# Sigmoid attention with an MLP behind it: prologue splits and maxima move off GpSimd, and float32 scores use 64 array rows per head

## The chip, the cores and the metric

The kernel runs on one core of a Trainium2 chip. The core has a matrix engine (TensorE, in the profile PE for the multiplications and PEld for its weight loads), VectorE (DVE), ScalarE (ACT), GpSimd (POOL) and SyncE (SP, which here only starts transfers). Each engine takes its own instructions in the order in which they were written down for it. The metric is the device time of one execution in microseconds; lower is better. The kernel before takes 1218.87 us (median of 3 runs, 1217.56 to 1221.67).

## The reference

```python
def _attn_ref(q, k, v):                 # q, k, v: (8, 12, 448, 64) float32
    scale = 1.0 / np.sqrt(q.shape[-1])
    scores = scale * np.matmul(q, k.transpose(0, 1, 3, 2)) - np.log(S)
    attn = 1.0 / (1.0 + np.exp(-scores))          # a sigmoid, no row sums
    return np.matmul(attn, v).astype(np.float32)

def _moe_ref(x, w_in, w_out):           # x: (3584, 768), w_in: 768 x 2048, w_out: 2048 x 768
    h = x @ w_in
    g = np.where(h >= 1, h, np.where(h <= -1, 0.0, (h + 1) ** 2 / 4))
    return (g @ w_out).astype(np.float32)
```

The attention output, transposed to (batch * seq, heads * head_dim), is `x`. Everything has to hold float32 accuracy. The weights arrive as float64.

## The kernel before, in words

**Blocks and pairs.** The work is cut into 8 blocks, one for each batch entry (448 tokens). Two heads make a pair, so a block has 6 pairs and the whole program 48. A pair is done in four pieces: three of 128 keys and one of 64 keys for both heads together (the "mid" piece). For a piece PE makes the scores (`psc`), ACT the sigmoid, and PE adds attention times v into `pav`. When a pair is done, `pav` is copied to `x32`, and VectorE takes its largest absolute value (`xm`).

**Precision.** Nearly every product is made of three float16 products: a number is scaled by a power of two, split into a high float16 part (ACT, a copy that rounds) and a low one (VectorE, scaled number minus high part), and the products high*high, low*high and high*low are added up. The scale comes from a maximum, or a sum that bounds it. Pairs 0 to 7 (`NFULL`) are multiplied in float32 without a split. Pairs 8 to 13 (`NHALF`) have q and k split and the rest in float32; later pairs are split throughout, and q, k and v each need a sum of absolutes, a scale and three GpSimd steps (lines 358 to 360): scale in place, round to the high part, subtract.

**Float32 pairs before the change.** The four buffers of `full` (`NFB = 4`) hold q for both heads on 128 partitions, v, and k twice: once with head 0 alone (the lower 64 partitions zeroed by a memset) and once with head 1 alone. A score matmul of one head therefore runs over 128 array rows, half of them multiplying by zero.

**Weights.** `w_in` and `w_out` come in 16 chunks of 128 x 768 each, as 64-bit words. `Weight.convert` makes float32 of one chunk: an absolute value on ACT (line 215), a lower clamp (line 217 on GpSimd, or line 225 on VectorE with the maximum taken on the way), then three bit operations on VectorE (lines 230, 233, 236). Where GpSimd clamps, a sum of absolutes on ACT (line 209) stands in for the maximum. `split` then makes the two float16 parts, either with ACT and VectorE (lines 275, 276) or with GpSimd scaling, ACT rounding and GpSimd subtracting (lines 271 to 273).

**MLP.** For a block, `up` (line 699) makes h chunk by chunk, `bend` applies the bent square and splits the result (ACT lines 712 and 715, VectorE lines 713, 714 and 716 (`GPOOL = 1` leaves the last on VectorE)), and `down` (line 733) multiplies by `w_out`. Block 0 and 1 do this plainly. From block 2 on (`SB = 2`) the up product goes through seven products of half size (`up_blocks`, line 665), whose weight combinations `mix` computes once, during block 1, and stores in DRAM (`blocks`); `load_set` brings them back.

**What sets the order.** The python code interleaves the pieces of the next block's attention with the MLP units of this one: `step(at)` issues piece `at`, `units` are the MLP units, and constants such as `WI_A`, `B0`, `LAST` and `MIX0` say at which unit which piece, weight chunk or mix step is written. A scheduler then orders each engine's instructions by its own estimate of times, with priorities lent by `tc.high_priority` (`WI_PRIO`, `X_PRIO`, `Q_PRIO`). Only the SP queue of the opening follows the written order. Block 0's MLP needs `finish_x(0)`: the largest of all six `xm`, a scale, and the split of `x32` (lines 500 and 501). For later blocks `start_blocks` and `finish_blocks` do the same at MLP unit `last`.

So there is an opening (weights converted and split, pairs 0 to about 17, the MLP of blocks 0 and 1, the mixing) and then a regular part, blocks 2 to 7.

Of the kernel before, what the change touches and what calls it, by code (L numbers as in the profile page):

```python
# [66 lines left out]
def sigmoid_attention_mlp(ctx: ExitStack, tc: tile.TileContext, first_qvk, qkv, w_in, w_out, out_t):  # L67
# [102 lines left out]
    class Weight:  # L170
# [30 lines left out]
        def convert(self):  # L201
# [11 lines left out]
            if f < NFC:  # L213
                a = self.f32(f)
                nc.scalar.activation(a, self.words_of(f)[1].bitcast(F32), AF.Abs)
                if f in self.summed:
                    nc.gpsimd.tensor_scalar(out=a, in0=a, scalar1=HIGH_MIN, scalar2=None, op0=ALU.max)
# [67 lines left out]
    NFB = 4  # L285
    full = ghl.rearrange("p f h n -> p (f h n)").bitcast(F32).rearrange("p (b t n) -> p b t n", b=NFB, t=4)
    for i in range(NFB):
        nc.vector.memset(full[D:, i, 2, :], 0.0)
        nc.vector.memset(full[:D, i, 3, :], 0.0)
# [47 lines left out]
    def prep_b(p):  # L337
        if not NFULL <= p < NPAIR or not first_time("split", p):
# [17 lines left out]
        for t, dst in enumerate(parts):  # L356
            rt, hi = r[:, t * S : 2 * S + VW if t == 2 else (t + 1) * S], dst[:, 0, :]
            nc.gpsimd.tensor_scalar(out=rt, in0=rt, scalar1=s[:, t : t + 1], scalar2=1.0, op0=ALU.mult, op1=ALU.mult)  # L358
# [14 lines left out]
    def scores(todo):  # L373

        tiles = []
        for i in todo:
# [5 lines left out]
            if p < NFULL:  # L382
                r = ready[p][0]
                for j in range(2):
                    out = psc[j * D : (j + 1) * D, 0, :S] if mid else psc[:, j, :S]
                    nc.tensor.matmul(out, r[:, 2 + j, w], r[:, 0, :], start=True, stop=True)  # L386
# [35 lines left out]
    def weigh(i, psc):  # L422
# [5 lines left out]
        sqk = 1.0 / math.sqrt(D) if p < NFULL else ready[p][2]  # L428
# [19 lines left out]
    def av(i):  # L448
# [30 lines left out]
        if mid:  # L479
            if p < NFULL + NHALF:  # L480
                nc.scalar.activation(x32[:, hp, :], pav[:, :S], AF.Copy)
            else:
# [1 line left out]
                nc.vector.tensor_scalar(
                    out=x32[:, hp, :], in0=pav[:, :S], scalar1=inv[:, 2:3], scalar2=1.0 / ATT, op0=ALU.mult, op1=ALU.mult
                )
# [450 lines left out]
```

## Time and profile before

| of the profiled execution | |
|---|---|
| its own time | 1220.22 us |
| its span (first to last instruction) | 1218.2 us |
| median of 3 other runs | 1218.87 us |
| busy PE, DVE, ACT, POOL | 1169.6, 883.8, 686.7, 495.5 us |
| first `up` matmul of block 0 (line 699) | at 88.45 us |
| first `up` matmul of block 1 (line 699) | at 242.27 us |
| first `up_blocks` matmul of block 2 (line 665) | at 428.36 us |

The last three rows are starts in the timeline and cut the span into stages; all stages below are taken between them. Busy time is the time in which at least one instruction of an engine ran. A matmul's recorded duration is longer than its share of the array's time, since consecutive matmuls overlap; start-to-start times tell what one costs.

### The profile page before, as it was taken

The numbers are of one execution on the slowest core, as the hardware profiler recorded it, in microseconds if no ns is written. First come the engines' busy times: TensorE is split into PE (matmuls) and PEld (weight loads), VectorE is DVE, ScalarE is ACT, GpSimd is POOL, SyncE is SP. The second block draws the span as 40 slices with busy tenths as digits, with TensorE's granted clock in tenths as the row PEclk, the third lists the DMA queues.
The fourth block names the chain that finished last, engine by engine and source line by source line (L and its number), as shares of the span: only waits on it lengthen the run. The fifth ranks groups of instructions, "written<-read, shape, count | busy, mean of one in ns | idle before, by whom it ended". The sixth has DMA issues, their size and how long they took to land.

```text
span 1218.2 us, 20267 instructions
## 1 busy us (share of the span) xinstructions
PE 1169.6 (96%) x7662; PEld 681.2 (56%) x7662; DVE 883.8 (73%) x1756; ACT 686.7 (56%) x1137; POOL 495.5 (41%) x508
## 2 busy tenths in 40 slices
PE   7978879999989999999999999999999999999998
PEld 2323333344444577556774577556774578557954
DVE  6879997799696479845985579845995579844830
ACT  6867657455464277743785377743785378621410
POOL 2567977555455134532354134532354234210000
PEclk9989989899999999999999999999999999999999
DMA  9844314414644136520654136520654136301400
GB/s 324 301 156 149 128 42 153 137 60 150 230 163 151 56 138 231 175 93 26 241 189 140 57 138 225 181 94 25 237 187 145 59 138 207 136 31 64 180 16 31
DMA packets 57217, 170.01 MB, mean 140 GB/s; under 512 B 8736, under 2 KB 37920, under 8 KB 50976
## 3 DMA queue, kind: packets, MB, share of 16 engines
q1 hardware_dynamic: 55392, 159.29, 38.1%
q10 hardware_dynamic: 1728, 9.44, 2.2%
q8 instruction: 60, 0.98, 0.3%
q14 instruction: 37, 0.30, 0.1%
HBM read 126.94 MB, written 23.40 MB: 123 GB/s over the span
## 4 chain that ended last, share of the span: by engine, by line
PE 70%; DVE 13%; POOL 7%; DMA 4%; issue 3%; ACT 2%; SPq 1%; POOLq 0%; ACTq 0%
PE po L733 31%; PE ph L665 22%; PE pav L475 8%; PE psc L395 3%; PE psc L386 2%; PE psc L404 2%; PE psc L390 1%; DVE g L713 1%; POOL w_in_sb L271 1%; DMA raw<-qkv 1%; DVE w_out_sb L233 1%; DVE ghl L716 1%; DVE mixs L623 1%; DMA blocks<-mixs 1%; POOL hl L360 1%
## 5 line engine op out<-in xcount | busy, mean ns | idle before, releaser
L733 PE MATMUL po<-ghl,w_out_sb 128*128 128x448 f16 x2304 | 451.5, 354 | 0.9 <-DVE g L714 0.5
L733 PEld LDWEIGHTS <-w_out_sb 128*128 128x128 f16 x2304 | 221.4, 98 | 222.7 <-issue 23.7
L665 PE MATMUL ph<-w_in_sb 128*128 128x224 f16 x3024 | 303.1, 259 | 1.5 <-DMA w_in_sb<-blocks 1.5
L665 PEld LDWEIGHTS <-w_in_sb 128*128 128x128 f16 x3024 | 285.4, 98 | 23.1 <-issue 17.3
L358 POOL TENSOR_SCALAR raw<-raw,qkv_s 128x448 f32<-128x448 f32 (+1 forms) x114 | 98.3, 874 | 434.6 <-DVE qkv_i L130 207.8
L434 ACT ACTIVATE psc<-psc,nls,sqk 128x896 f32<-128x896 f32 (+1 forms) x136 | 129.5, 971 | 131.2 <-PE psc L404 121.3
L443 DVE SCALAR_TENSOR_TENSOR ahl<-psc,ahl 128x896 f16<-128x896 f32 (+1 forms) x170 | 152.8, 899 | 49.7 <-ACT ahl L442 47.5
L442 ACT ACTIVATE ahl<-psc 128x896 f16<-128x896 f32 (+1 forms) x170 | 125.9, 765 | 37.0 <-DVE ahl L443 35.0
L699 PE MATMUL ph<-xhl,w_in_sb 128*128 128x448 f16 x576 | 120.3, 368 | 9.6 <-DVE g L714 8.0
L743 DVE TENSOR_SCALAR o<-po,od 128x448 f32<-128x448 f32 x48 | 32.6, 681 | 108.5 <-PE po L733 107.7
L475 PE MATMUL pav<-ahl,v 128*64 128x448 f16 x748 | 101.1, 366 | 0.0
L674 DVE TENSOR_TENSOR xhl<-ph,xhl 128x224 f32<-128x224 f32 x240 | 88.0, 384 | 17.7 <-PE ph L665 13.7
L699 PEld LDWEIGHTS <-w_in_sb 128*128 128x128 f16 x576 | 57.1, 101 | 77.9 <-issue 30.4
L332 ACT ACTIVATE dump<-raw 128x448 f16<-128x448 f32 (+1 forms) x108 | 63.6, 589 | 65.4 <-DMA raw<-qkv 62.9
L716 DVE TENSOR_TENSOR ghl<-g,ghl 128x448 f16<-128x448 f32 x128 | 91.0, 726 | 6.3 <-ACT ghl L715 5.9
L715 ACT ACTIVATE ghl<-g 128x448 f16<-128x448 f32 x128 | 72.4, 571 | 35.9 <-DVE g L714 35.0
L360 POOL TENSOR_TENSOR hl<-raw,hl 128x448 f16<-128x448 f32 x80 | 89.3, 1134 | 0.0
L713 DVE SCALAR_TENSOR_TENSOR g<-g,rk 128x448 f32<-128x448 f32 x112 | 84.3, 771 | 2.9 <-ACT g L712 2.2
L712 ACT ACTIVATE g<-xhl,hr,ihr 128x448 f32<-128x448 f32 x96 | 67.9, 753 | 31.9 <-DVE xhl L674 31.5
L395 PE MATMUL psc<-qk 128*128 128x448 f16 x252 | 67.6, 356 | 5.9 <-DVE ahl L443 4.3
L386 PE MATMUL psc<-ghl 128*128 128x448 f32 (+1 forms) x128 | 53.7, 596 | 12.7 <-ACT a L431 6.9
L714 DVE SCALAR_TENSOR_TENSOR g<-xhl,ihs,g 128x448 f32<-128x448 f32 x96 | 63.0, 677 | 0.0
(167 smaller groups left out, 1312.7 us busy)
## 6 DMA issues: line engine op xcount, KB each, us to landing
w_in_sb<-blocks SPq DMA_DIRECT2D x48, 1344.0 KB, 6.3
raw<-qkv SPq DMA_DIRECT2D x34, 704.0 KB, 6.8
qk<-hl SPq DMA_DIRECT2D x320, 56.0 KB, 2.0
w_out_sb<-w_in SPq DMA_DIRECT2D x16, 768.0 KB, 9.4
out_t<-o SPq DMA_DIRECT2D x48, 224.0 KB, 1.9
blocks<-mixs SPq DMA_DIRECT2D x8, 768.0 KB, 4.3
w_out_sb<-w_out ACTq DMA_DIRECT2D x6, 768.0 KB, 4.2
raww<-w_out ACTq DMA_DIRECT2D x6, 768.0 KB, 5.1
```

The lines of the kernel that those rows point to most:

```text
L358: nc.gpsimd.tensor_scalar(out=rt, in0=rt, scalar1=s[:, t : t + 1], scalar2=1.0, op0=ALU.mult, op1=ALU.mult)
L360: nc.gpsimd.tensor_tensor(out=dst[:, 1, :], in0=rt, in1=hi, op=ALU.subtract)
L395: nc.tensor.matmul(out, kq[:, j, 1, w], kq[:, j, 0, :], start=True, stop=False)
L434: nc.scalar.activation(a, a, AF.Sigmoid, bias=nls, scale=sqk)
L442: nc.scalar.activation(hi, x, AF.Copy, scale=ATT)
L443: nc.vector.scalar_tensor_tensor(out=lo, in0=x, scalar=ATT, in1=hi, op0=ALU.mult, op1=ALU.subtract)
L475: nc.tensor.matmul(pav[j * D : (j + 1) * D, :S], *terms[j][t], start=c == 0 and t == 0, stop=mid and t == len(terms[j]) - 1,)
L665: nc.tensor.matmul(out, w[:, wt, wh, c * P : (c + 1) * P], xc[:, xt, c, xh, :], start=j in (0, 2) and c + wh + xh == 0, stop=c == HC - 1 a ...
L699: nc.tensor.matmul(ph[:, :S], w_in_sb[:, f, wh, c * P : (c + 1) * P], xhl[:, c, xh, :], start=c == 0 and wh + xh == 0, stop=c == NCC - 1 a ...
L713: nc.vector.scalar_tensor_tensor(out=g, in0=g, scalar=rt, in1=g, op0=ALU.min, op1=ALU.mult)
L716: (nc.gpsimd if f % GPOOL else nc.vector).tensor_tensor(out=ghl[:, f, 1, :], in0=g, in1=hi, op=ALU.subtract)
L733: nc.tensor.matmul(po[:, :S], w_out_sb[:, f, wh, m * P : (m + 1) * P], ghl[:, f, gh, :], start=f == lo and wh + gh == 0, stop=f == hi - 1 ...
```

## The change

1. **Float32 scores.** `full` has five buffers of three parts (q, v, k) without zeros; a head's scores now take its own 64 partitions of k and q, that is 64 array rows. The memsets go, and a pair is loaded by two transfers where it was three.
2. **Off GpSimd.** In the opening the clamps of `w_in` from chunk 7 on go to VectorE (`CLAMP`). `WO_SUM = 0`: all `w_out` chunks take maximum and clamp in one VectorE instruction (line 236 of the new kernel), without ACT's sum. `POOL_FROM = 6` and `WOP = 6`: `w_in` chunks 4 to 7 and five `w_out` chunks more are split by ACT and VectorE. The q, k and v of pairs 8 to 16 (`QA`) are split by ACT and VectorE, two instructions in place of three. The two additions of each `mix` go to VectorE (`MIXP = 0`).
3. **x32.** For split pairs the copy out of `pav` goes from VectorE to ACT; its factor is made by one tiny VectorE instruction for each pair.
4. **Order.** `LAST` 84 (the regular blocks spread their attention over more MLP units, and `finish_blocks` comes six units later), other times and priorities in the opening, and `down` from block 2 on takes chunks u and u + 8 together.

```diff
-LAST = 78
+LAST = 84
-WI_B = 9
+WI_B = 5
-POOL_FROM = 2
+POOL_FROM = 6
-WO_SUM = 1
-MAX_ACT = 48
+WO_SUM = 0
+MAX_ACT = 47
-MIX0 = 4
+MIX0 = 8
-Q_PRIO = 60
+Q_PRIO = 72
-WI_PRIO = 132
+WI_PRIO = 280
...
-                    nc.gpsimd.tensor_scalar(out=a, in0=a, scalar1=HIGH_MIN, scalar2=None, op0=ALU.max)
+                    (nc.vector if f >= CLAMP else nc.gpsimd).tensor_scalar(
+                        out=a, in0=a, scalar1=HIGH_MIN, scalar2=None, op0=ALU.max
+                    )
...
-            r = full[:, p % NFB]
-            nc.sync.dma_start(out=r[:D, 2, :], in_=first_qvk[p, :D, 2, :])
-            nc.sync.dma_start(out=r[D:, 3, :], in_=first_qvk[p, D:, 2, :])
-            nc.sync.dma_start(out=r[:, 0:2, :], in_=first_qvk[p, :, 0:2, :])
+            r = full[:, slot_of(p)]
+            nc.sync.dma_start(out=r[:, ::2, :], in_=first_qvk[p, :, ::2, :])
+            nc.sync.dma_start(out=r[:, 1, :], in_=first_qvk[p, :, 1, :])
...
+            if p < QA and t != QT:
+                nc.scalar.activation(hi, rt, AF.Copy, scale=s[:, t : t + 1])
+                nc.vector.scalar_tensor_tensor(
+                    out=dst[:, 1, :], in0=rt, scalar=s[:, t : t + 1], in1=hi, op0=ALU.mult, op1=ALU.subtract
+                )
+                continue
...
-                    nc.tensor.matmul(out, r[:, 2 + j, w], r[:, 0, :], start=True, stop=True)
+                    rows = slice(j * D, (j + 1) * D)
+                    nc.tensor.matmul(out, r[rows, 2, w], r[rows, 0, :], start=True, stop=True)
...
-                nc.vector.tensor_scalar(
-                    out=x32[:, hp, :], in0=pav[:, :S], scalar1=inv[:, 2:3], scalar2=1.0 / ATT, op0=ALU.mult, op1=ALU.mult
-                )
+                sv = ready.pop(p)[2][:, 1:2]
+                nc.scalar.activation(x32[:, hp, :], pav[:, :S], AF.Copy, scale=sv)
...
-            nc.gpsimd.tensor_tensor(out=a[:, r], in0=w_in_sb[:, chunk, 0, :], in1=w_in_sb[:, chunk, 1, :], op=ALU.add)
+            (nc.gpsimd if r < MIXP else nc.vector).tensor_tensor(
+                out=a[:, r], in0=w_in_sb[:, chunk, 0, :], in1=w_in_sb[:, chunk, 1, :], op=ALU.add
+            )
...
-        for f in range(lo + 2 * u, lo + 2 * u + 2):
+        pair = (u, u + NFC // 2) if b >= SB else (lo + 2 * u, lo + 2 * u + 1)
+        for f in pair:
...
-                wo.split(split_at, split_at % 2 == 1)
+                wo.split(split_at, split_at % WOP == 1)
```

The scheduler's order moves with it. The first place is GpSimd in the opening. Before, from its first clamp on (line 217 clamps, 271 and 273 split weights, 358 to 360 split q and k; the number behind x counts equal neighbours):

```order
L217 TENSOR_SCALAR w_in_sb<-w_in_sb 128x768 x6
L271 TENSOR_SCALAR w_in_sb<-w_in_sb,wi_s 128x768 x3
L358 TENSOR_SCALAR raw<-raw,qkv_s 128x448 x2
L271 TENSOR_SCALAR w_in_sb<-w_in_sb,wi_s 128x768
L359 TENSOR_SCALAR hl<-raw 128x448 x2
L217 TENSOR_SCALAR w_in_sb<-w_in_sb 128x768
L360 TENSOR_TENSOR hl<-raw,hl 128x448 x2
L358 TENSOR_SCALAR raw<-raw,qkv_s 128x448 x2
L359 TENSOR_SCALAR hl<-raw 128x448 x2
L360 TENSOR_TENSOR hl<-raw,hl 128x448
L217 TENSOR_SCALAR w_in_sb<-w_in_sb 128x768
L360 TENSOR_TENSOR hl<-raw,hl 128x448
```

Now, from its first clamp (line 226) on, up to the split of pair 17, the first pair that it still splits:

```order
L226 TENSOR_SCALAR w_in_sb<-w_in_sb 128x768 x4
L282 TENSOR_SCALAR w_in_sb<-w_in_sb,wi_s 128x768 x8
L284 TENSOR_TENSOR w_in_sb<-w_in_sb 128x768 x8
L434 MEMSET w_in_sb 128x256 x2
L282 TENSOR_SCALAR w_out_sb<-w_out_sb,wo_s 128x768 x2
L284 TENSOR_TENSOR w_out_sb<-w_out_sb 128x768 x2
L282 TENSOR_SCALAR w_out_sb<-w_out_sb,wo_s 128x768
L284 TENSOR_TENSOR w_out_sb<-w_out_sb 128x768
L437 COPY w_in_sb<-hl 64x2x64 x6
L378 TENSOR_SCALAR raw<-raw,qkv_s 128x448 x2
```

These few rows are nearly all that GpSimd does in the opening now; before, the piece shown is only its beginning.

The second place is VectorE just ahead of `finish_x(0)`, whose split of x (line 501) block 0's `up` waits for. Before (line 236 the last bit operation of a chunk, 276 a weight split, 487 the maximum of a finished pair, 496 the maximum over the block):

```order
L487 TENSOR_REDUCE xm<-x_91 128x1
L236 SCALAR_TENSOR_TENSOR w_in_sb<-w_out_sb,w_in_sb 128x768 x2
L276 SCALAR_TENSOR_TENSOR w_in_sb<-w_in_sb,wi_s 128x768
L230 TENSOR_SCALAR w_in_sb<-w_in_sb 128x768
L233 SCALAR_TENSOR_TENSOR w_in_sb<-w_out_sb,w_in_sb 128x768
L276 SCALAR_TENSOR_TENSOR w_in_sb<-w_in_sb,wi_s 128x768
L236 SCALAR_TENSOR_TENSOR w_in_sb<-w_out_sb,w_in_sb 128x768
L487 TENSOR_REDUCE xm<-x_91 128x1
L496 TENSOR_REDUCE xm_523<-xm 128x1
```

Now (236 is the combined clamp and maximum, 241, 244 and 247 are the bit operations, 287 a weight split, 508 and 517 the maxima):

```order
L244 SCALAR_TENSOR_TENSOR w_out_sb<-w_out_sb 128x768 x2
L262 TENSOR_SCALAR wi_x<-wi_m 128x1
L287 SCALAR_TENSOR_TENSOR w_in_sb<-w_in_sb,wi_s 128x768
L236 TENSOR_SCALAR w_out_sb,wo_most<-w_out_sb 128x768
L247 SCALAR_TENSOR_TENSOR w_out_sb<-w_out_sb 128x768 x2
L265 SCALAR_TENSOR_TENSOR wi_x<-wi_m,wi_x 128x1
L241 TENSOR_SCALAR w_out_sb<-w_out_sb 128x768
L287 SCALAR_TENSOR_TENSOR w_in_sb<-w_in_sb,wi_s 128x768
L236 TENSOR_SCALAR w_out_sb,wo_most<-w_out_sb 128x768
L269 TENSOR_SCALAR wi_x<-wi_x,wi_m 128x1
L508 TENSOR_REDUCE xm<-x_91 128x1
```

Before, VectorE was still converting `w_in` here; now `w_out` chunks are under way ahead of `finish_x(0)`. Counted over the whole order ahead of the last instruction of that split: 15 chunks' bit operations became 20, 8 combined maxima 12, 5 weight splits 9, and 4 clamps and 4 splits of q or k are new. In the regular part the largest of a block's x is taken to `finish_blocks` 66 `down` matmuls ahead of the next block where it was 102.

More of the change, by code (lines that the diff above doesn't have):

```diff
@@ L45 @@
 B0 = 9
-B1 = 64
+B1 = 66
 GPOOL = 1
-POOL_FROM = 2
+POOL_FROM = 6
 WI_SUM = 2
-WO_SUM = 1
-MAX_ACT = 48
+WO_SUM = 0
+MAX_ACT = 47
 L0 = 9
-A0 = 17
-LSTEP = 1
+A0 = 19
+LSTEP = 3
 SB = 2
-MIX0 = 4
+CLAMP = 7
+QA = 17
+QT = 3
+WOP = 6
+MIXP = 0
+CORN = 10
+TP = 1
+DW = 8
+MIX0 = 8
 MIX1 = 85
-Q_PRIO = 60
+Q_PRIO = 72
 PM = 9
-WI_PRIO = 132
+WI_PRIO = 280
 X_PRIO = 593
@@ L282, in sigmoid_attention_mlp, with slot_of @@
     NPAIR = B * NP
[L285 to L289, printed above, removed]
+    NFB = 5
+    full = ghl.rearrange("p f h n -> p (f h n)").bitcast(F32)[:, : NFB * 3 * S]
+    full = full.rearrange("p (b t n) -> p b t n", b=NFB, t=3)
+    def slot_of(p):
+        return (p + 2) % NFB
     done = set()
@@ L344, in prep_b @@
         s, inv = scales(m, n, "qkv")
-        sqk = sml_p.tile([P, 1], F32, tag="sqk", name="sqk")
+        sqk = sml_p.tile([P, 2], F32, tag="sqk", name="sqk")
+        if n == 3:
+            nc.vector.tensor_scalar(out=sqk[:, 1:2], in0=inv[:, 2:3], scalar1=1.0 / ATT, scalar2=None, op0=ALU.mult)
         nc.vector.tensor_scalar(
-            out=sqk, in0=inv[:, 0:1], scalar1=inv[:, 1:2], scalar2=1.0 / math.sqrt(D), op0=ALU.mult, op1=ALU.mult
+            out=sqk[:, 0:1], in0=inv[:, 0:1], scalar1=inv[:, 1:2], scalar2=1.0 / math.sqrt(D), op0=ALU.mult, op1=ALU.mult
         )
@@ L415, in scores @@
                     rows = slice(j * D, (j + 1) * D)
-                    nc.gpsimd.tensor_copy(out=corner(p)[rows, :, rows], in_=ready[p][4][rows, 1, :, NKC * P :])
+                    (nc.vector if p < CORN else nc.gpsimd).tensor_copy(
+                        out=corner(p)[rows, :, rows], in_=ready[p][4][rows, 1, :, NKC * P :]
+                    )
     def corner(p):
@@ L427, in weigh @@
         a = psc[:, :n, :S]
[L428 removed]
+        sqk = 1.0 / math.sqrt(D) if p < NFULL else ready[p][2][:, 0:1]
         if p < NFULL + NHALF:
@@ L843, in sigmoid_attention_mlp @@
         f, r = divmod(u, NCC // 2)
+        assert all(at >= NPC * (p + 1) or (f + 1) * S * 4 <= slot_of(p) * 3 * S * 4 for p in range(NP, NFULL)), u
         if r == 0 and f < NFC:
@@ L874, in sigmoid_attention_mlp @@
         first = at
+        share = [DW if b < SB or u < len(units) - 48 else 8 for u in range(last)]
+        share = [sum(share[:u]) / sum(share) for u in range(last + 1)]
         with ExitStack() as order:
@@ L878, in sigmoid_attention_mlp @@
             for u, unit in enumerate(units):
-                while at < min(b + 2, B) * NPIECE and (at - first) * (last - 1) // NPIECE <= u:
+                while at < min(b + 2, B) * NPIECE and (at - first) < share[min(u + 1, last)] * NPIECE:
                     step(at)
@@ L883, in sigmoid_attention_mlp @@
                     while split_at < min(NFC, NA + (u + 1) * (NFC - NA) // (NA * NCC // 2 - 2)):
-                        wo.split(split_at, split_at % 2 == 1)
+                        wo.split(split_at, split_at % WOP == 1)
                         split_at += 1
```

6 lines of the change are left out of this document (3 added, 3 removed).

## The prediction

> **What bounds the kernel now.** I read the busy times by stage first, then VectorE's and GpSimd's groups in the opening with what VectorE waited for, last PE's timeline. The busy times of the five stages, cut where the first `up` matmuls of blocks 0, 1 and 2 start (columns: length, then busy us and instructions of each engine, granted clock, DMA share, GB/s):
>
> ```profile
> 0.00:88.40 88.40, 75.41 (x240) 26.22 (x241) 67.45 (x116) 59.46 (x87) 43.97 (x32) 0.96 0.75 255
> 88.40:242.20 153.80, 136.22 (x629) 55.70 (x627) 135.55 (x236) 97.85 (x159) 111.13 (x74) 0.92 0.38 127
> 242.20:370.00 127.80, 117.71 (x622) 54.80 (x622) 116.35 (x193) 71.66 (x117) 73.60 (x65) 0.97 0.42 146
> 370.00:428.40 58.40, 56.56 (x309) 27.72 (x307) 29.93 (x71) 21.15 (x34) 16.94 (x20) 0.97 0.33 112
> 428.40:1218.20 789.80, 783.72 (x5869) 516.77 (x5867) 534.52 (x1143) 436.59 (x744) 249.84 (x318) 1.00 0.38 130
> ```
>
> The last row is the regular part: PE is busy 99% of 789.8 us, so moving work between the other engines can give nothing there. Up to 370 us VectorE is busy 319.35 us; in the second and third stages 88% and 91%, and GpSimd, at 228.70 us, runs beside it most of that time. From 370 to 428 PE has its dense `down` and VectorE is half idle. So the 370 us are a VectorE stage with PE close behind, and the change is won or lost in them.
>
> VectorE's groups to 428.4 us (count, busy us, mean ns, idle before). Below them three of its operations with shortest/median/longest ns:
>
> ```profile
> L716 DVE TENSOR_TENSOR ghl<-g,ghl 128x448 f16<-128x448 f32 x32 | 27.9, 872 | 1.6 <-ACT ghl L715 1.5
> L714 DVE SCALAR_TENSOR_TENSOR g<-ph,ihs,g 128x448 f32<-128x448 f32 x32 | 21.6, 675 | 0.2
> L713 DVE SCALAR_TENSOR_TENSOR g<-g,ru 128x448 f32<-128x448 f32 x16 | 17.5, 1097 | 0.0
> L236 DVE SCALAR_TENSOR_TENSOR w_in_sb<-w_out_sb,w_in_sb 128x768 int32<-128x768 int32 x16 | 17.3, 1085 | 0.1
> L233 DVE SCALAR_TENSOR_TENSOR w_in_sb<-w_out_sb,w_in_sb 128x768 int32<-128x768 int32 x16 | 16.9, 1055 | 0.2
> L230 DVE TENSOR_SCALAR w_out_sb<-w_out_sb 128x768 int32<-128x768 int32 x16 | 15.0, 939 | 3.5 <-POOL w_out_sb L217 3.5
> L713 DVE SCALAR_TENSOR_TENSOR g<-g,rk 128x448 f32<-128x448 f32 x16 | 14.3, 898 | 0.0
> L501 DVE SCALAR_TENSOR_TENSOR xhl<-x,x_s,xhl 128x448 f16<-128x448 f32 x12 | 13.4, 1130 | 0.0
> L230 DVE TENSOR_SCALAR w_in_sb<-w_in_sb 128x768 int32<-128x768 int32 x16 | 11.8, 743 | 11.7 <-POOL w_in_sb L217 11.7
> ```
> ```profile
> L716 DVE TENSOR_TENSOR ghl<-g,ghl x32: 608/614/2121, 109.6 to 370.3; 128x448 f16<-128x448 f32 x32
> L230 DVE TENSOR_SCALAR w_out_sb<-w_out_sb x16: 544/555/2004, 97.6 to 214.6; 128x768 int32<-128x768 int32 x16
> L236 DVE SCALAR_TENSOR_TENSOR w_in_sb<-w_out_sb,w_in_sb x16: 945/958/1605, 13.7 to 95.2; 128x768 int32<-128x768 int32 x16
> ```
>
> Lines 713 and 714 are the same operation on the same size, back to back. 714, one of whose inputs is in PSUM, takes 675 ns; 713, both inputs in SBUF, 1097 in block 0 and 898 in block 1. What differs by input and by stage is GpSimd beside it. Busy time less count times the undisturbed duration: 8.4 us for 716, 10.2 for 713, 4.0 for the two 768-column rows, 9.3 for 230, 5.3 for 501; 37 us in these rows, and by the same subtraction over the groups not shown some 75 us of VectorE's time to 428 us is waiting on GpSimd inside the instructions. This is the quantity that the change can release.
>
> **The change, part by part.** First what GpSimd loses, from its groups over the same stretch:
>
> ```profile
> L217 POOL TENSOR_SCALAR w_out_sb<-w_out_sb 128x768 f32<-128x768 f32 x14 | 36.6, 2628 | 11.2 <-ACT w_out_sb L215 11.1
> L360 POOL TENSOR_TENSOR hl<-raw,hl 128x448 f16<-128x448 f32 x24 | 30.2, 1271 | 0.0
> L611 POOL TENSOR_TENSOR mixa<-w_in_sb 128x768 f32<-128x768 f16 x16 | 27.5, 1739 | 31.8 <-DVE qkv_e L124 10.1 <-DMA out_t<-o 7.2 <-DVE ghl L716 7.0
> L358 POOL TENSOR_SCALAR raw<-raw,qkv_s 128x448 f32<-128x448 f32 x24 | 23.6, 995 | 37.9 <-DVE qkv_i L130 37.8
> L273 POOL TENSOR_TENSOR w_in_sb<-w_in_sb 128x768 f16<-128x768 f32 x12 | 22.4, 1865 | 17.8 <-ACT w_in_sb L272 17.8
> L359 POOL TENSOR_SCALAR hl<-raw 128x448 f16<-128x448 f32 x24 | 18.5, 782 | 0.0
> L271 POOL TENSOR_SCALAR w_in_sb<-w_in_sb,wi_s 128x768 f32<-128x768 f32 x12 | 16.5, 1390 | 1.0 <-DVE wi_i L130 1.0
> ```
>
> All 14 `w_out` clamps go (36.6) and 4 of the 8 of `w_in` (10.5 at the same mean); all mix additions (27.5); 18 of 24 q and k splits (0.75 of 72.3 = 54.2) and 3 v splits (at the q and k steps' means 9.1); 9 weight splits (9 x (1.39 + 1.87) = 29.3). That is 167 of the four stages' 245.6 us; a third remains.
>
> What VectorE gains, undisturbed: 14 clamps with maximum at 0.95 (row below), 13.3; 4 plain clamps at 230's 0.55, 2.2; 9 weight splits at 236's 0.95, 8.6; 21 q, k and v splits at 714's 0.68, 14.3; 16 mix additions, whose duration no row shows, between 230's 0.55 and 236's 0.95, so 8.8 to 15.2, taken at the top because like 236 they read two tensors. Tiny factors for pairs add about 2, and four `x32` copies leave (0.67 each, row below). Together 46 to 53, taken as 53. ACT loses 14 sums (line 209) and gains 21 q, k and v roundings and four copies, all well under 1 us each; with 250 busy of 428 us it has room.
>
> ```profile
> L225 DVE TENSOR_SCALAR_CACHE_REDUCE w_in_sb<-w_in_sb x8: 937/947/954, 14.6 to 87.1; 128x768 f32<-128x768 f32 x8
> L484 DVE TENSOR_SCALAR x<-pav,qkv_i x34: 669/672/685, 316.0 to 1079.5; 128x448 f32<-128x448 f32 x34
> DVE w_in_sb L230 <- POOL w_in_sb L217: 11.7, 4, 6.5
> DVE mixa L613 <- POOL mixa L611: 6.4, 2, 4.2
> DVE w_out_sb L230 <- POOL w_out_sb L217: 3.5, 3, 2.0
> ```
>
> What VectorE gets back: if the loss of 75 us shrinks as GpSimd's busy time does, two thirds, 50 us; the bounds are nothing and all 75. Its open waits for GpSimd are the last three rows (us in total, times, longest). Of their 21.6 us, 6.5 is the very first chunk, which GpSimd still clamps; I take 14 of the other 15. About 45 instructions more, each starting some 0.06 us before the end of its predecessor as the rows do now, need 3 less than their durations say. Net: 53 - 50 - 14 - 3 = **-14 us** for the opening.
>
> The stages inside it differ in sign. Ahead of `finish_x(0)` VectorE's queue now holds five more chunks' bit operations (5 x 2.4 = 12), 4 maxima (3.8), 4 clamps (2.2), 4 weight splits (3.8) and 4 half splits (2.7): 24.5 us more, less some 8 us of slowdown, 3 of clamp waits and 1.5 of overlap. So block 0's `up` starts about 12 us later, near 100 us, and the rest up to block 2 falls from 340 to about 314.
>
> The float32 scores: PE's timeline, one scores-and-values round after another (start, duration, x records; a float32 matmul is two records):
>
> ```profile
> 18.09 0.97 PE L475 MATMUL pav<-a,ghl 128*64 128x448 f32 x4
> 18.99 1.77 PE L386 MATMUL psc<-ghl 128*128 128x448 f32 x4
> 20.69 0.97 PE L475 MATMUL pav<-a,ghl 64*64 64x448 f32 x4
> 21.59 2.67 PE L386 MATMUL psc<-ghl 128*128 128x448 f32 x8
> ```
>
> Scores on 128 x 128 of the array take 1.70 start to start, two matmuls in turn. The values on 64 x 64, two heads on rows and columns of their own, take 0.90 for the same four records: the heads run together. Scores on 64 rows by 128 columns have no float32 row; the bounds are 1.70 (no overlap, plus two mode changes) and 0.90, and I take 0.90. That is 24 pieces x 0.80 = 19 us less PE work, nearly all ahead of block 0's `up`. It goes on the path nowhere: PE already idles 13 us in the first stage and would wait there for `finish_x(0)` till about 100 us. Worth: 0.
>
> A longer wait has a price, though. After such a wait this happened:
>
> ```profile
> 76.74 1.76 PE L386 MATMUL psc<-ghl 128*64 128x448 f32 x4 [3.80 <-ACT a L431]
> ```
>
> Four records, 0.97 us for the values above, took 1.76 behind an idle time of 3.8 us: half clock. The Trainium skill, "TensorE: Matmul & The Clock Gate", section "HAM oscillation — how this bites in real kernels", warns of PE gaps beyond about 3 us, after which the clock falls to half until the array has been busy for a window again; the trace agrees. By that rule the wait ahead of block 0's `up` costs one such window, an estimate of under 2 us, and the sum would be -12 in place of -14 us.
>
> The regular part: the `x32` copy moves from VectorE to ACT, both idle over 30% there; `finish_blocks` comes 36 `down` matmuls later:
>
> ```profile
> 544.15 19.46 PE L733 MATMUL po<-ghl,w_out_sb 128*128 128x448 f16 x102
> 551.73 0.91 DVE L527 SCALAR_TENSOR_TENSOR w_in_sb<-x,x_s,w_in_sb 128x672 f16<-128x672 f32 x1
> 566.15 1.03 PE L665 MATMUL ph<-w_in_sb 128*128 128x224 f16 x9
> ```
>
> The last split of x ends 13.5 us ahead of its first reader; 36/102 of 19.46 us is 6.9, so 6.6 us of cover are left. Cost 0, if ACT's copy is not held up by more than that. The new `down` order takes late chunks late; PE shows no wait there to win back.
>
> **Rivals.** (1) *The slowdown does not shrink with GpSimd's work.* What GpSimd keeps, eight weight splits in a row, runs just beside block 0's `bend` chains. If only 25 us came back, VectorE would have 53 - 25 - 14 - 3 = 11 us more: 1230. It decides below 36 us back. Rows 713 speak for it (1097 in the stage with most GpSimd work), 898 in the next speaks for proportion.
> (2) *PE sets the start of block 0 after all.* Should the scheduler's order let `finish_x(0)` come right behind pair 5, the delay of 12 us is not incurred, and of the 14 us that the scores of six pairs save (6 x 3 x 0.80) a third may arrive: -14 - 12 - 5 = -31, 1188. Against it, VectorE's queue ahead of it, 67.45 us busy before.
> (3) *Nothing is won:* the waits for GpSimd come back as waits for ACT, which now rounds before each VectorE subtraction, 12 us of them: 1217.
> (4) *The scores do not overlap.* PE gets its 19 us back and two mode changes a piece; behind VectorE that still costs little, time as forecast.
>
> **How the numbers follow.** The profiled execution took 1220.22 us, 1.35 over the median. 1220.2 - 14 = 1206; against the median 1218.87 - 14 = 1205. Chances: the forecast (gain of 4 to 27 us, rival 4 within it) 0.58; (2) or otherwise more than 27 us 0.13; (3) 0.14; (1) or another loss 0.15. A change under 0.3%, 3.7 us, can hardly be told from none: faster 0.71, same 0.14, slower 0.15. The range 1186 to 1224 goes from rival 2 to the milder half of rival 1; the forecast's own is 1192 to 1215.
>
> **What would show it.** Line 713's successor (736) near 0.75 us in block 0, GpSimd near 80 us busy up to block 2, four score records in about 0.97 us, the first `up` later than 88.45 us with PE idle ahead of it, the first `up_blocks` near 414, and block lengths behind that as before. I am wrong if 736 stays near 1.1 us, if VectorE shows new waits for ACT of over 10 us, if `up` starts by 80 us, or if the regular part moves by more than 3 us.

## The result and the profile after

The changed kernel takes **1190.29 us** (median of 4 runs, 1187.38 to 1193.08) against 1220.27 us for the kernel before on the same chip: ratio 0.9755, 95% interval 0.9722 to 0.9788. It is 30 us faster; the forecast was 14 us, 1205. The profiled execution took 1187.38 us, the shortest of the four.

The busy times by stage, cut again at the first `up` matmuls of blocks 0 and 1 (now line 722) and the first `up_blocks` matmul of block 2 (line 688); columns as in the prediction:

```profile
0.00:91.70 91.70, 67.59 (x252) 17.94 (x252) 78.34 (x149) 68.59 (x99) 9.66 (x10) 0.91 0.76 279
91.70:223.50 131.80, 124.40 (x627) 52.72 (x626) 124.38 (x259) 85.33 (x132) 30.91 (x23) 1.00 0.39 128
223.50:394.40 170.90, 167.54 (x919) 81.74 (x918) 133.67 (x279) 98.62 (x162) 37.72 (x42) 0.99 0.44 145
394.40:1185.70 791.30, 785.35 (x5869) 516.91 (x5867) 518.54 (x1143) 445.01 (x768) 254.52 (x318) 1.00 0.38 130
```

The regular part is 1.5 us longer, so the whole gain lies ahead of 394 us. The first stage grew by 3.3 us, the second shrank from 153.9 to 131.8, the third (370 to 428 us of before included) from 186.1 to 170.9. GpSimd's busy time fell from 245.6 to 78.3 us. VectorE's, although it took over most of that work, fell from 349.3 to 336.4 us and its idle time from 79 to 58. PE's idle time behind the first stage fell from 29.5 to 10.8 us: from 92 to 394 us PE is busy 96% of the time, though in the second stage VectorE is as busy (124.4 us).

VectorE's groups up to 394.4 us (737 is the old 714, 736 the old 713, 739 the old 716; 632 and 374 are moved work):

```profile
L737 DVE SCALAR_TENSOR_TENSOR g<-ph,ihs,g 128x448 f32<-128x448 f32 x32 | 21.6, 676 | 0.1
L739 DVE TENSOR_TENSOR ghl<-g,ghl 128x448 f16<-128x448 f32 x32 | 20.6, 650 | 1.6 <-ACT ghl L738 1.6
L632 DVE TENSOR_TENSOR mixa<-w_in_sb 128x768 f32<-128x768 f16 x16 | 14.7, 958 | 2.3 <-DMA blocks<-mixs 2.3
L736 DVE SCALAR_TENSOR_TENSOR g<-g,ru 128x448 f32<-128x448 f32 x16 | 12.9, 811 | 0.7 <-ACT g L735 0.7
L736 DVE SCALAR_TENSOR_TENSOR g<-g,rk 128x448 f32<-128x448 f32 x16 | 12.3, 771 | 0.3 <-ACT g L735 0.3
L374 DVE SCALAR_TENSOR_TENSOR hl<-raw,qkv_s,hl 128x448 f16<-128x448 f32 x18 | 11.8, 680 | 0.3 <-ACT hl L373 0.3
```

Line 736 with both inputs in SBUF takes 811 and 771 ns where it took 1097 and 898, and 739 takes 650 where it took 872; 737, with an input in PSUM, is at 676 as it was at 675. That is what the Trainium skill states in "SBUF — State Buffer", section "Who interferes with whom": a VectorE instruction contends with a GpSimd instruction that reads SBUF only where it takes two inputs from SBUF or runs in a two-port mode. The trace agrees, by these three lines, and record by record: of the 32 instructions of line 713 in the kernel before, the 21 that overlap a GpSimd instruction take 1168 ns on average, the other 11 673 and none over 679, while those of 714 take 674 and 676. By the subtraction that the prediction used, VectorE now loses some 25 us to GpSimd where it lost 78 (2 or 3 us more or less, by what is taken as undisturbed).

PE's timeline in the opening; scores (line 407) now run on 64 of the array's rows:

```profile
16.24 0.97 PE L498 MATMUL pav<-a,ghl 128*64 128x448 f32 x4
17.14 1.02 PE L407 MATMUL psc<-ghl 64*128 64x448 f32 x4
18.10 0.97 PE L498 MATMUL pav<-a,ghl 128*64 128x448 f32 x4
```

Four score records take 0.96 us start to start (17.14 to 18.10), for 1.70 before.

VectorE's waits up to 394.4 us (us in total, times, longest):

```profile
DVE w_in_sb L241 <- POOL w_in_sb L226: 10.7, 2, 10.1
DVE o L768 <- PE po L758: 8.9, 2, 8.3
DVE ahl L466 <- ACT ahl L465: 8.7, 3, 4.6
```

Of the waits for GpSimd only the one for the first chunk's clamp stays. The wait of `ahl` for ACT was 3.4 us before; its cost is looked at below.

PE's waits between the first `up` and the first `up_blocks`, before:

```profile
PE ph L699 <- DVE g L714: 8.0, 5, 2.2
PE pm L166 <- DVE g L714: 6.3, 2, 4.7
PE psc L395 <- DVE ahl L443: 3.3, 2, 2.0
```

and after:

```profile
PE ph L722 <- DVE g L737: 3.4, 3, 1.8
PE pm L159 <- DVE g L737: 3.2, 2, 2.6
```

Most of PE's waits before were for VectorE, and they are halved or gone: a faster VectorE reaches the end through them.

The moves did a second thing. The chain of work that ended last, followed back from the end of the execution to what released each step, runs in the kernel before through GpSimd's own instructions for 83 of the opening's 428 us (VectorE 157, PE 114). A piece of it in the first stage (start, duration):

```profile
64.40 2.33 POOL hl L360 x2
66.74 3.81 POOL raw L358 x2
70.54 1.76 POOL hl L359 x2
72.30 1.71 POOL hl L360
74.01 2.81 POOL w_in_sb L217
```

In the changed kernel GpSimd holds 5 us of that chain. So the moves released VectorE's slowdown and also took GpSimd's own time off the path. The releasers are inferred from the profile, and no run below parts the two.

### The profile page after: what moved, and what is told of

Read it like the earlier page. It is cut to its first block, busy times and chain, and to the rows that moved or that the text cites. A ratio compares the mean times of both kernels' runs of the same rounds, so it can differ in the third digit from the quotient of the medians.

```text
span 1185.7 us, 20268 instructions
## 1 busy us (share of the span) xinstructions
PE 1144.9 (97%) x7662; PEld 669.3 (56%) x7662; DVE 854.9 (72%) x1828; ACT 697.6 (59%) x1158; POOL 332.8 (28%) x393
## 4 chain that ended last, share of the span: by engine, by line
PE 71%; DVE 17%; DMA 4%; ACT 3%; issue 2%; POOL 2%; SPq 0%; POOLq 0%; ACTq 0%; DVEq 0%
PE po L758 33%; PE ph L688 22%; PE pav L498 8%; PE psc L416 3%; PE psc L425 2%; PE ph L722 2%; DVE g L736 2%; PE psc L411 1%; DVE g L737 1%; DVE ghl L739 1%; DMA raw<-qkv 1%; DVE ahl L466 1%; DVE w_in_sb L244 1%; DVE mixa L632 1%; DVE w_out_sb L247 1%
## 5 line engine op out<-in xcount | busy, mean ns | idle before, releaser
L758 PE MATMUL po<-ghl,w_out_sb 128*128 128x448 f16 x2304 | 446.3, 353 | 1.5 <-DVE qkv_e L131 0.6
L688 PE MATMUL ph<-w_in_sb 128*128 128x224 f16 x3024 | 307.7, 259 | 1.3 <-DVE g L737 0.9
L688 PEld LDWEIGHTS <-w_in_sb 128*128 128x128 f16 x3024 | 282.6, 98 | 30.1 <-issue 27.2
L378 POOL TENSOR_SCALAR raw<-raw,qkv_s 128x448 f32<-128x448 f32 (+1 forms) x93 | 71.0, 777 | 449.9 <-DVE qkv_i L139 346.3
L722 PE MATMUL ph<-xhl,w_in_sb 128*128 128x448 f16 x576 | 114.5, 356 | 4.7 <-DVE g L737 3.4
L498 PE MATMUL pav<-ahl,v 128*64 128x448 f16 x748 | 95.6, 360 | 0.0
L722 PEld LDWEIGHTS <-w_in_sb 128*128 128x128 f16 x576 | 55.7, 99 | 63.6 <-issue 14.4
L739 DVE TENSOR_TENSOR ghl<-g,ghl 128x448 f16<-128x448 f32 x128 | 85.0, 672 | 5.3 <-ACT ghl L738 4.8
L380 POOL TENSOR_TENSOR hl<-raw,hl 128x448 f16<-128x448 f32 x62 | 71.1, 1167 | 0.0
L737 DVE SCALAR_TENSOR_TENSOR g<-xhl,ihs,g 128x448 f32<-128x448 f32 x96 | 66.3, 708 | 0.3
L498 PEld LDWEIGHTS <-v 128*64 128x64 f16 x748 | 36.3, 109 | 37.9 <-issue 23.0
```

Of the source, the lines that this page charges most:

```text
L498: nc.tensor.matmul(pav[j * D : (j + 1) * D, :S], *terms[j][t], start=c == 0 and t == 0, stop=mid and t == len(terms[j]) - 1,)
L688: nc.tensor.matmul(out, w[:, wt, wh, c * P : (c + 1) * P], xc[:, xt, c, xh, :], start=j in (0, 2) and c + wh + xh == 0, stop=c == HC - 1 a ...
L722: nc.tensor.matmul(ph[:, :S], w_in_sb[:, f, wh, c * P : (c + 1) * P], xhl[:, c, xh, :], start=c == 0 and wh + xh == 0, stop=c == NCC - 1 a ...
L737: nc.vector.scalar_tensor_tensor(out=g, in0=h, scalar=ihs, in1=g, op0=ALU.mult, op1=ALU.max)
L739: (nc.gpsimd if f % GPOOL else nc.vector).tensor_tensor(out=ghl[:, f, 1, :], in0=g, in1=hi, op=ALU.subtract)
L758: nc.tensor.matmul(po[:, :S], w_out_sb[:, f, wh, m * P : (m + 1) * P], ghl[:, f, gh, :], start=f == lo and wh + gh == 0, stop=f == hi - 1 ...
```

## The experiments

Twelve kernels. Columns: median; ratio to the kernel before with its 95% interval; lengths of the three stages of the opening and of the regular part in the profiled execution; PE's idle time in stages two and three; GpSimd's busy time in the opening (all us).

| kernel | median | ratio | one / two / three / regular | PE idle | GpSimd |
|---|---|---|---|---|---|
| before | 1218.6 to 1220.5 | 1 | 88.4 / 153.9 / 186.1 / 789.8 | 29.5 | 245.6 |
| after | 1190.29 | 0.9755 (0.9722 to 0.9788) | 91.7 / 131.8 / 170.9 / 791.3 | 10.8 | 78.3 |
| b_moves | 1203.03 | 0.9852 (0.9831 to 0.9873) | 92.1 / 147.1 / 176.9 / 788.7 | 20.6 | 75.8 |
| b_scores64 | 1225.54 | 1.0048 (1.0029 to 1.0067) | 101.2 / 144.0 / 189.3 / 789.3 | 29.7 | 235.0 |
| a_scores128 | 1210.91 | 0.9936 (0.9916 to 0.9957) | 93.3 / 146.1 / 179.4 / 790.2 | 29.2 | 74.5 |
| a_samerows | 1198.28 | 0.9819 (0.9780 to 0.9857) | 96.6 / 131.5 / 172.5 / 790.5 | 10.8 | 78.4 |
| a_poolback | 1227.44 | 1.0070 (1.0049 to 1.0090) | 105.1 / 139.2 / 191.9 / 790.8 | 29.2 | 234.9 |
| a_qkvpool | 1211.12 | 0.9927 (0.9912 to 0.9941) | 93.4 / 139.4 / 185.8 / 791.2 | 24.0 | 138.9 |
| a_mixpool | 1197.99 | 0.9821 (0.9805 to 0.9837) | 92.9 / 133.3 / 179.6 / 790.5 | 17.9 | 106.0 |
| a_oldorder | 1205.83 | 0.9890 (0.9867 to 0.9913) | 100.3 / 136.7 / 179.2 / 789.4 | 15.4 | 78.8 |
| a_x32dve | 1189.23 | 0.9746 (0.9729 to 0.9764) | 93.2 / 132.9 / 172.9 / 789.1 | 11.0 | 77.1 |
| b_fill | 1219.14 | 1.0006 (0.9989 to 1.0023) | 87.5 / 151.8 / 187.6 / 788.4 | 32.1 | 247.0 |
| b_moves_fill | 1199.58 | 0.9830 (0.9808 to 0.9852) | 89.2 / 140.6 / 177.9 / 789.0 | 17.0 | 75.9 |
| a_fill | 1189.51 | 0.9749 (0.9731 to 0.9767) | 94.2 / 131.8 / 172.8 / 790.1 | 12.1 | 78.6 |

### One part undone, or one part alone

**a_scores128**, the changed kernel with the old score buffers (four of four parts, zeros, three loads a pair):

```diff
...
-                    nc.tensor.matmul(out, r[rows, 2, w], r[rows, 0, :], start=True, stop=True)
+                    nc.tensor.matmul(out, r[:, 2 + j, w], r[:, 0, :], start=True, stop=True)
```

> The changed kernel with its float32 scores back on 128 array rows (four buffers with zeroed halves, three loads a pair); all else as changed. VectorE theory (the gain of 30 us is VectorE's lost slowdown in the opening, the scores lie beside its queue): within 4 us of the changed kernel, 1186 to 1195; block 0's up still starts near 92 us. PE theory (the shorter scores bring a good part): 12 to 19 us more, 1202 to 1209, and block 0's up starts over 10 us later.

Measured: 20.6 us slower than after. The first stage is only 1.6 us longer; 14.3 are lost in the second and 8.5 in the third. The first `up` matmul of block 0, what VectorE does ahead of it, and the second stage's row:

```profile
93.34 0.90 PE L724 MATMUL ph<-xhl,w_in_sb 128*128 128x448 f16 x2 [8.44 <-ACT xhl L523]
...
84.68 0.28 DVE L176 TENSOR_REDUCE xm<-pm 128x1 f32<-128x128 f32 x1
...
91.68 0.15 DVE L135 TENSOR_SCALAR x_s<-x_e 128x1 int32<-128x1 int32 x1
...
93.30:239.40 146.10, 126.78 (x620) 53.90 (x620) 131.60 (x268) 87.90 (x134) 29.51 (x23) 0.94 0.37 125
```

PE stands 8.4 us ahead of block 0's `up` for the split of x. The maximum over x (line 176) is there at 85.0 us, but eight instructions of weight conversion and splitting stand between it and its scale (line 135), which comes 7 us later. In after the same two steps are 0.7 us apart, with nothing large between them:

```profile
89.29 0.29 DVE L176 TENSOR_REDUCE xm<-pm 128x1 f32<-128x128 f32 x1
...
89.99 0.15 DVE L135 TENSOR_SCALAR x_s<-x_e 128x1 int32<-128x1 int32 x1
```

In the second stage VectorE has 131.6 us of work where after has 124.4: three of the eight mixes instead of two stand ahead of block 1's `up`, and PE waits for VectorE for 12.7 us instead of 5.2. The scheduler, reckoning with longer scores, laid down another order. So this run alone does not tell what the overlap of the pieces is worth.

**b_scores64**, the kernel before with the new score buffers alone:

```diff
...
-                    nc.tensor.matmul(out, r[:, 2 + j, w], r[:, 0, :], start=True, stop=True)
+                    rows = slice(j * D, (j + 1) * D)
+                    nc.tensor.matmul(out, r[rows, 2, w], r[rows, 0, :], start=True, stop=True)
```

> The kernel before with the 64-row scores alone. VectorE theory: no change, 1216 to 1224, since the wait for the split of x takes up what the scores save. PE theory: 12 to 19 us less, 1201 to 1208.

Measured: about 6 us slower than before. Block 0's `up` starts at 101.2 us, with 82.1 us of VectorE's busy time ahead of it instead of 67.5. Without the moves the scores win nothing.

**a_poolback**, the changed kernel with all moves off GpSimd undone (the constants are put on one line here, and in the next two edits):

```diff
-CLAMP, WO_SUM, POOL_FROM, QA, WOP, MIXP = 7, 0, 6, 17, 6, 0
+CLAMP, WO_SUM, POOL_FROM, QA, WOP, MIXP = 99, 1, 2, 0, 2, 2
```

> The changed kernel with clamps, weight splits, q, k and v splits and mix additions back on GpSimd as before; 64-row scores, x32 on ScalarE and the new order constants stay. VectorE theory: nearly the whole gain goes, 1212 to 1224, and the line of g with both inputs in SBUF goes back from 0.79 to about 1.0 us. Order theory (the constants bring it): half or more of the gain stays, 1190 to 1205. PE theory: 1200 to 1207.

Measured: 37 us slower than after, and slower than before. The whole gain needs the moves; the other parts without them are a loss of 8 to 9 us.

**a_oldorder**, the changed kernel with eight of the old places and priorities; the new rule that spreads the pieces over the units, `MAX_ACT` and the new order of `down` stay:

```diff
-LAST, WI_B, B1, A0, LSTEP, MIX0, Q_PRIO, WI_PRIO = 84, 5, 66, 19, 3, 8, 72, 280
+LAST, WI_B, B1, A0, LSTEP, MIX0, Q_PRIO, WI_PRIO = 78, 9, 64, 17, 1, 4, 60, 132
```

> The changed kernel with eight order constants of before (LAST, WI_B, B1, A0, LSTEP, MIX0 and two priorities). VectorE theory: 1188 to 1198, since the work on each engine is that of the changed kernel. Order theory: most of the gain goes, 1205 to 1220.

Measured: 15.5 us slower than after. Its first stage:

```profile
0.00:100.30 100.30, 68.97 (x237) 17.73 (x238) 80.56 (x154) 67.17 (x98) 9.66 (x10) 0.80 0.67 248
```

Block 0's `up` starts at 100.3 us, where the forecast had put it for the changed kernel; the new places take 8.6 us off that, and 4.9 and 8.3 off the next stages.

**b_moves**, the kernel before with the moves off GpSimd and nothing else:

```diff
-POOL_FROM, WO_SUM = 2, 1
+POOL_FROM, WO_SUM, QA, QT = 6, 0, 17, 3
-        nc.gpsimd.tensor_tensor(out=a[:, r], in0=w_in_sb[:, chunk, 0, :], in1=w_in_sb[:, chunk, 1, :], op=ALU.add)
+        nc.vector.tensor_tensor(out=a[:, r], in0=w_in_sb[:, chunk, 0, :], in1=w_in_sb[:, chunk, 1, :], op=ALU.add)
...
```

> The kernel before with the moves from GpSimd alone: q, k and v low parts, the maxima of chunks 7 and up, the sums for w_out, five of six late w_out splits and the mixes' sums on VectorE and ScalarE; scores on 128 rows, the old places and the old x32 copy stay. VectorE theory (the forecast's): the slowdown beside GpSimd of 77.8 us falls by about 50 and pays for the moved work, so the moves alone give the forecast's gain or more: 1200 to 1208 against 1218.6. Needs-each-other theory: undoing the scores (20.6 us), the places (15.5 us) and the moves (37 us) costs 73 us together where the change gave 28, so each is worth little without the others: 1214 to 1222, with the slowdown gone but VectorE's and TensorE's waits in the first two stages up by as much.

Measured: 17.5 us faster than before (four runs from 1200.65 to 1206.52; the profiled execution is the longest of them). The stages:

```profile
0.00:92.10 92.10, 77.36 (x256) 27.02 (x257) 75.13 (x148) 70.34 (x101) 10.12 (x10) 0.96 0.79 278
92.10:239.20 147.10, 131.72 (x621) 54.45 (x621) 130.55 (x266) 84.17 (x130) 31.13 (x23) 0.92 0.35 114
239.20:416.10 176.90, 171.66 (x920) 82.24 (x920) 138.28 (x279) 96.68 (x158) 34.57 (x42) 0.97 0.42 141
```

VectorE's time lost beside GpSimd is some 26 us, as in the changed kernel, and GpSimd holds 2 us of the chain. This is the part on which the forecast was built, alone, and near the forecast's size. The other 13 us come from scores and places together (the new spreading of the pieces and `MAX_ACT`, which no run undoes, counted with the places): in the changed kernel with the old scores the places are a loss (1210.9 against 1203.0; the `x32` copy, which differs too, is worth nothing, see below), with the old places the scores are none of use (1205.8), with both it is 1190.3.

**a_mixpool and a_qkvpool**, the changed kernel with one move undone each:

```diff
-MIXP = 0
+MIXP = 2
```
```diff
-QA = 17
+QA = 0
```

> The changed kernel with the mixes' 16 sums on GpSimd again (in the kernel with all moves undone 6 of 11.2 us in the second stage and 10 of 17.5 us in the third; on VectorE they take 15.3 us). Slowdown theory: 29 us of GpSimd work slow VectorE by some 9 us and take 15 us from it, so VectorE's sum falls by 6; the second and third stages are bound by TensorE, with 7.4 and 3.4 us of idle time, so the time is the same, 1187 to 1194. Chain theory: the unmixing waits 0.7 us longer for each sum and the first up_blocks matmul comes later by up to 8 us: 1195 to 1200.

> The changed kernel with one of the moves undone: the splits of q, k and v of pairs 0 to 5 run on GpSimd again (scale, high and low parts; some 36 of the 157 us of GpSimd work that undoing all moves brings back before the first up_blocks matmul, with 12 low parts less on VectorE, 8 us). Slowdown theory: all the moves cost 37 us for 157 us of GpSimd work, so in proportion 8 us: 1196 to 1201, VectorE's slowdown up by 10 to 15 us in the three stages, less 8 us of work. Chain theory: what counts is that the q, k and v of a pair are ready sooner, because TensorE waits for them (scores of a pair start only when its four steps on GpSimd, 0.9 to 1.3 us each, are done): 1205 or more, with TensorE waiting for hl written on GpSimd in the first two stages.

Measured: 7.7 us slower for the mixes' sums, 20.8 us for q, k and v (of pairs 8 to 16; the expectation names the wrong pairs, and the work brought back was 60.6 us, not 36). The first lost its time in the third stage, where line 736 is slow again beside GpSimd's sums (2.8 us more in all, of 8.7):

```profile
L736 DVE SCALAR_TENSOR_TENSOR g<-g,rk 128x448 f32<-128x448 f32 x16 | 15.1, 941 | 0.0
226.20:405.80 179.60, 170.93 (x919) 82.23 (x918) 137.46 (x267) 99.39 (x163) 58.19 (x54) 0.97 0.42 139
```

The second lost it in the second and third:

```profile
93.40:232.80 139.40, 129.85 (x627) 53.38 (x626) 128.33 (x244) 83.83 (x126) 56.11 (x47) 0.96 0.39 127
232.80:418.60 185.80, 171.39 (x922) 82.65 (x921) 134.66 (x276) 92.17 (x151) 58.33 (x69) 0.96 0.39 129
```

Both came out at the chain theory's time, but in neither trace is a part split on GpSimd among PE's listed waits in the stages that lost. VectorE's lost time rose from 25 to some 39 and 43 us and ate up what it had been relieved of (busy 337 and 343 us in the opening, 336 in after), and PE stood idle longer, 17.9 and 24.0 us for 10.8. That fits the slowdown, but does not show it alone: GpSimd holds 33 us of the chain in a_qkvpool, 25 of them in these splits, and 8 in a_mixpool, for 5 in after. The order changes with these edits too; VectorE's is that of the changed kernel only for its first 325 (a_mixpool) and 75 (a_qkvpool) of 685 instructions. In the three kernels that give work back to GpSimd, 27.7, 60.6 and 156.6 us of it cost 7.7, 20.8 and 37 us: 0.24 to 0.34 us for each. With the old scores and places the same moves brought 17.5 us for 170, 0.10.

**a_x32dve**, the changed kernel with the `x32` copy back on VectorE:

```diff
-                nc.scalar.activation(x32[:, hp, :], pav[:, :S], AF.Copy, scale=sv)
+                nc.vector.tensor_scalar(out=x32[:, hp, :], in0=pav[:, :S], scalar1=sv, scalar2=1.0, op0=ALU.mult, op1=ALU.mult)
```

> The changed kernel with the scaled copies of the attention's output into x32 on VectorE again instead of ScalarE. The forecast put this part of the change at 0 us: 1188 to 1193. Order theory: another order is laid down on every engine (20,688 lines of difference on TensorE), and each of the orders tried with one part undone cost 8 to 21 us: 1195 to 1210, with more of TensorE's waits and more spells at half clock between the first up and the first up_blocks matmul.

Measured: 1 us faster than after, no difference that can be told. This says little on the order theory, though: up to 292 us VectorE's order is that of the changed kernel, for 536 of its 689 instructions in the opening, and PE's is up to 311 us.

### The order kept

**a_samerows**, the changed kernel with both heads of a float32 pair read from the same 64 rows, so that the pieces cannot run beside each other; the second head's own scores are left out. Each engine's instructions stand as in the changed kernel:

```diff
-                    rows = slice(j * D, (j + 1) * D)
+                    rows = slice(0, D)
```

> The changed kernel, with one edit: both heads of a float32 score pair are read from rows 0 to 63, so the two pieces of a pair cannot run beside each other (the second head's scores are then computed from the first head's rows). Every engine's instructions stand in exactly the order of the changed kernel. Order theory: putting the scores back on 128 rows cost 20.6 us because the scheduler then laid down another order (the unmixing chain and the six maxima of x's columns come earlier or later, TensorE waits 8.4 us at one place for a copy of xhl); here the order is kept, so the time stays within 6 us of the changed kernel's 1190, and TensorE's extra work in the first stage goes into its 24.1 us of idle time there. Work theory: the kernel is TensorE-bound from 92 us on, so the 24 pieces that no longer overlap, 0.8 us each, are 19 us of which most reach the end: 1202 to 1209, the first up matmul of block 0 at 92 to 105 us and the later stages as before.

Measured: 8 us slower than after by the medians, with a wide spread (1192.86 to 1203.19; the two 95% intervals of the ratio, up to 0.9788 and from 0.9780 on, just touch); the profiled execution, at 1192.86, is 5.5 us over that of after. PE's timeline and its first stage:

```profile
51.16 1.77 PE L407 MATMUL psc<-ghl 64*128 64x448 f32 x4
0.00:96.60 96.60, 90.39 (x253) 28.71 (x254) 78.72 (x149) 69.00 (x99) 9.67 (x10) 1.00 0.73 265
```

The four records take 1.77 us again. PE has 22.8 us more to do in the first stage, its idle time there falls from 24.1 to 6.2 us, its clock there is 1.00 where it was 0.91, and block 0's `up` comes 4.8 us later (in a_x32dve, whose order up to there is after's, it comes 1.5 us later by chance); the later stages are as in after. So most of the saved score work falls into PE's idle time, as forecast, and some 5 to 8 us of it reach the end, by this small difference. If the parts add up, the other 12 to 15 of the 20.6 us of a_scores128 are the order, the old loads and the zeros.

**The clock.** In the opening of before PE runs at half clock for 3.4 or 6.8 us after several of its waits, which costs 17 us of PE time between 88 and 428 us (one less the granted clock, times the length of each stage, unrounded clocks); in b_moves it is 16.8, in after 1.7. That looked like the missing 13 us. Three kernels test it by empty matmuls (identity times 64 columns, into PSUM columns that nothing reads), put into PE's order ahead of the matmuls that wait, after the order was laid down; all else stands as it stood:

```diff
...
+            for _ in range(count):
...
+                nc.tensor.matmul(spare, ident, few, start=start, stop=start)
...
```

> The kernel before, nothing moved, with 253 empty matmuls put into nine of TensorE's waits between 135 and 351 us in the same way. Clock theory: five spells at half clock (from 150, 174, 218, 259 and 321 us, 27.2 us in all) go, which is worth up to 13.6 us of TensorE's time: 1206 to 1212 against 1219.5, though VectorE's slowdown stays. Wait theory: VectorE sets the pace of these stages, the time is the same, 1217 to 1223.

> The kernel before with the moves alone (1203.0 us), and 210 empty matmuls of 64 columns put ahead of the matmuls for which TensorE waits longest there (65 ahead of the first up matmul of block 0, 34 ahead of its fourth, 30 at 212 us, 43 ahead of the first of block 1, 38 at 338 us); they go to unused columns of PSUM and every other instruction stands as it stood. Clock theory: each of these waits (2.4 to 5.2 us) is followed 1 to 3 us later by 3.4 to 13.7 us at half clock, 30.7 us in all, which cost 15.4 us of TensorE's time; with TensorE kept busy they go, and the time falls by 8 to 15 us, to 1188 to 1195, with the granted clock of the stages from the first up matmul near 1.0. Wait theory: TensorE waits for VectorE and ScalarE all the same, and what the clock loses it would have waited: 1201 to 1206 whatever the clock does. If an empty matmul takes well over 0.08 us, up to 5 us are lost.

> The changed kernel with 82 empty matmuls in four of its waits (at 61, 141, 223 and 239 us). It has one spell at half clock of 3.4 us left after the first up matmul (from 241 us): clock theory 1.7 us less, 1187 to 1190; wait theory no change, 1190.

In **b_fill** the loss to the clock fell from 17.1 to 3.4 us and the time stayed, 1219.14 against 1218.71 us:

```profile
87.50:239.30 151.80, 133.13 (x783) 58.23 (x782) 135.63 (x239) 96.67 (x158) 111.54 (x74) 0.99 0.38 127
239.30:426.90 187.60, 174.19 (x1027) 85.02 (x1026) 148.47 (x263) 93.87 (x152) 91.48 (x85) 0.99 0.40 137
```

One place shows why. PE's timeline in before, a little into block 1 (start, duration; in brackets the wait ahead):

```profile
258.25 5.25 PE L699 MATMUL ph<-xhl,w_in_sb 128*128 128x448 f16 x18 [2.15 <-DVE g L714]
...
276.21 2.81 PE L699 MATMUL ph<-xhl,w_in_sb 128*128 128x448 f16 x14 [0.59 <-DVE g L714]
```

and with 27 empty matmuls in that wait:

```profile
254.32 0.95 PE L936 MATMUL pav<-ident 128*128 128x64 bf16 x27
256.62 3.56 PE L699 MATMUL ph<-xhl,w_in_sb 128*128 128x448 f16 x18 [1.35 <-DVE g L714]
...
274.57 4.49 PE L699 MATMUL ph<-xhl,w_in_sb 128*128 128x448 f16 x14 [2.27 <-DVE g L714]
```

The 18 matmuls take 3.56 us instead of 5.25; 1.7 us won, and the next wait for VectorE grows from 0.59 to 2.27. What the clock lost, PE would have waited. (Behind the longer wait the clock halved in turn, for 3.4 us: the 14 matmuls take 4.49 us instead of 2.81.) In **b_moves_fill** the granted clock of the second stage rises only from 0.92 to 0.96, the loss behind the first `up` falls from 16.8 to 8.5 us, and the time falls by 3.5 us, which the two intervals hardly tell from nothing; in **a_fill** nothing changes. The wait theory holds for before and after. For b_moves, from which the 13 us are counted, it is not settled: if the 15 us by which it loses more to the clock than after were worth as much as the 8.3 that came back, they would be 6 us, an estimate.

## Why the prediction was right or wrong

- **The time.** 1190.3 lies in the range of 1186 to 1224, but only at its lower end, which was taken from rival 2; the forecast's own, 1192 to 1215, missed it.
- **VectorE sets the opening, PE the rest.** Right for the rest: the regular part kept its length (789.8 to 791.3), in all fourteen kernels within 3 us. In the opening VectorE has the largest part of the chain, 157 of 428 us; that GpSimd itself has 83 the prediction did not weigh, beyond VectorE's 14 us of waits for it.
- **GpSimd's slowdown of VectorE.** Right: forecast 75 us less 50, measured some 78 less 52 in the changed kernel, the same with the moves alone. Rival 1 is out. GpSimd's 78.3 us is the forecast's "near 80", line 736's 811 ns in block 0 a little over its 0.75 us.
- **VectorE's new work.** Forecast 53 us, measured 50 (the mix additions at 958 ns were at the upper bound as assumed, the splits at 680). With the slowdown that is 2 us less, yet VectorE was busy 13 us less: its instructions overlap the one before them by 49 us in all where it was 39, 10 us more where the forecast had put 3.
- **Waits.** Forecast 14 us less; VectorE's wait for GpSimd fell by 11, and its whole idle time by 21, since it waited less for PE as well. The new wait for ACT that was to prove the forecast wrong did not come: its largest row, `ahl`, went from 3.4 to 8.7 us, all of VectorE's waits for ACT from 21 to 25, and PE stood idle for only 3.4 of the third stage's 170.9 us, so rival 3 is out too.
- **The sum.** -14 us for the moves: the moves alone gave -17.5. The forecast had all of it in waits; in the moves' profiled execution VectorE's busy time fell by 5 us and its idle time by 7.
- **Stages.** Forecast: `up` of block 0 near 100 us, the first `up_blocks` near 414. Measured 91.7 and 394. With the old places it is 100.3 and 416: the step that failed is having given the new places and priorities no term. They are worth 15.5 us in this kernel, 8.6 of it ahead of block 0; with the old scores they are a loss of 8.
- **The scores, worth 0.** A term mis-sized: some 5 to 8 us with the order kept. Idle time of PE in the first stage does hide most of the saved work. It is not the wait for `finish_x(0)` that the prediction named, though: PE's 24.1 us lie earlier, most of them in waits for ACT's sigmoids (14.4 us). Once the moves had left PE 11 us of idle time behind the first stage, what made `up` late was no longer hidden.
- **Rival 2** (1188) had the nearer terms, a delay of `up` of 3.3 us and not 12, and 5 to 8 us of the scores, and a part of its mechanism, that PE sets the start of block 0: from 80.16 us to `up` at 91.74 PE runs without a wait and the chain goes through it but for 1 us, and with more score work `up` comes later. From 60 to 74 us the chain is VectorE's, so PE sets only the last stretch.
- **The clock rule.** By the rule of the Trainium skill's "TensorE: Matmul & The Clock Gate", section "HAM oscillation — how this bites in real kernels", the longer wait ahead of `up` was to cost under 2 us. Neither came: PE has no wait in the last 11.6 us ahead of `up`, and the clock of the second stage is 1.00.
- **x32, 0.** Right, 1189.2 against 1190.3.

What stays open: of the 13 us beyond the moves, some 5 to 8 are the overlap of the score pieces. The rest is put down to the order, which scores and places change together, with an unsettled part of it in the clock; a_scores128 shows one place of the order (weight conversion between the maximum over x and its scale), but no run took that alone. Nor did a run part VectorE's slowdown beside GpSimd from GpSimd's own time on the chain; both went with the moves.
